# Seven packed blocks and a ring that grows, for six blocks and a fixed ring

## The chip, the core and the metric

The kernel runs on one core of a Trainium2 chip. A core has a matrix engine (PE, TensorE), a vector engine (DVE, VectorE), a scalar engine (ACT, ScalarE), GpSimd (POOL) and a sync engine (SP), and 16 DMA engines that move data between HBM and the on-chip memory SBUF. All DMAs of this kernel are issued from the queues of SP (loads) and of ACT (stores). The metric is the device time of one execution in microseconds (us).

## The reference

The input x has 384 x 384 positions of 384 channels in bf16, 113.25 MB. The kernel needs the mean and the maximum of every channel over all positions, passes both through a small two-layer network, and multiplies x by the sigmoid of the result:

```python
xf = x.reshape(B, H * W, C)
gap = jnp.mean(xf, 1)
gmp = jnp.amax(xf, 1)
h_a = gap @ w1;  h_a = h_a * (h_a > 0)
h_m = gmp @ w1;  h_m = h_m * (h_m > 0)
scale = sigmoid(h_a @ w2 + h_m @ w2)
return x * scale[:, None, None, :]
```

The scale is known only when all of x has been read, and x does not fit in SBUF. So x is read once for mean and maximum (pass one), and what could not be kept is read again, multiplied and stored (pass two).

## The kernel before

The 147,456 positions are spread over the 128 partitions, 1152 on each. "A row" is one of those 1152: 384 channels, 768 B on each partition, 98,304 B over all. Blocks are stretches of consecutive rows, and a partition's part of a block is contiguous in HBM.

**Pass one.** `steps` lists loads and work in order, and one loop issues them in that order on every engine; nothing reorders them (`manual_schedule`). For each load, PE adds the rows up by matmuls with a column of ones (`sums`, L253), and VectorE takes the running maximum in `acc`, in pieces of 6 and 5 rows (`maximum`, L319). Most loads go to a ring of three slots of 39 rows (`SLOT`, `SLOTS`). A slot is loaded anew when VectorE and PE are both done with its last content, and as SP issues in order, a load that waits for its slot holds back all loads behind it.

**Packed blocks.** Six blocks of 32 rows (`PACKED`, `G = 8`: four parts of 8 rows) are kept in the place of 24 rows. The low bytes of the third and fourth part move to where the high bytes of the first and second were, and the high bytes of all four are squeezed to four bits each: matmuls with scaled identity matrices write them as 16-bit words into PSUM, and ScalarE evicts those words into the third part. For each block, in two halves, the order is: load 24 rows into `homes[i]` and 8 rows into `fourth[i]`, `test` (ScalarE, L280 and L281: do the values fit four bits?), `pack` first half (24 matmuls L301, two ScalarE copies L307, an eviction L308), more `test`, the first fill between the blocks, and then `pack` second half. PE's second pack needs the eviction of the first, because both use the PSUM tile `words`. `BETWEEN` says which fills of the slots come after each block (108 rows, so 140 with the block), `PASSING` which come after all blocks, and `judge` turns the tests into one flag. If a value did not fit, the packed rows are read again at the very end (`tc.If(bad != 0)`); with these inputs that is not taken.

**What stays.** The last loads of pass one remain in place: 120 rows in the slots (`STAYING`), 21 in `held` (`LAST_HELD`), and 18 in PSUM. Together with 192 packed rows, pass two has to read 790 rows again (`AGAIN`), and 8 + 11 rows of `held` and `acc` while the scale is computed.

**Pass two.** The rows that stayed are multiplied and stored in small pieces (`FIRST_STORES`). The 120 rows of the ring become four places of 30 rows (`PLACE`); as a place's rows have been stored, SP reads the next 30 into it. A turn is: multiply one place (L416), store it from ACT's queue (L469), issue the read that follows in the same place (L492), and do one job of `jobs`: unpack half a block (VectorE L447 and L452, then six ScalarE copies L466) or multiply a finished block (`finish`). Block 0 is stored as soon as it is finished and its place is used as scratch; blocks 1 to 5 stay in `room` and are stored in the last three turns and after them.

Two orders matter for what follows. Stores are issued from ACT's queue, so a store stands behind the ScalarE copies of the job before it. And the DMA completions are counted on eight semaphores in rotation: a DMA waits for the one eight before it in the program.

Of the kernel before, what the change touches and what calls it, by code (L numbers as in the profile page):

```python
# [12 lines left out]
BF16 = mybir.dt.bfloat16  # L13
# [14 lines left out]

SLOT = 39
SLOTS = 3
RING = 120
PLACE = 30
G = 8
PACKED = 6
PSUM_ROWS = 8
LATE_ROWS = 8
BANK_ROWS = 2
# [1 line left out]
HELD_ROWS = 21  # L41
# [2 lines left out]

FIRST_LOAD = 4
FOLD_BEFORE = 2
BETWEEN = ((18, 36, 33),) + ((36, 36, 36),) * 4 + ((38, 37, 33),)
PASSING = (31, 29, 26, 23, 16, 22, 16)
SHARED_FILL = 4
STAYING = {0: (11, 17, 11), 1: (14, 13, 12), 2: (11, 9, 6, 5, 6, 5)}  # L50
LAST_HELD = (5, 4, 6, 6)

AGAIN = (30,) * 26 + (10,)
FIRST_STORES = ((1, 2, 3, 4, 4, 6, 6, 6, 7), (12, 13, 14), (20, 22))
HELD_STORES = (6, 7)
ACC_STORES_AT = 3
TEST_SCALE = 0.031187
# [5 lines left out]
def kernel(  # L63
# [7 lines left out]
    nc = tc.nc  # L71
    P = nc.NUM_PARTITIONS
# [4 lines left out]
    TOT = HW // P  # L77
# [19 lines left out]
    def take(n):  # L97
        nonlocal at
        at += n
        return at - n, n  # L100
# [10 lines left out]
    assert at == TOT and sum(AGAIN) == n_pass and sum(LAST_HELD) == HELD_ROWS  # L111
    at = passing_at
    again = [take(n) for n in AGAIN]


    small = consts.tile([P, 16], BF16)
# [22 lines left out]
    ring = xpool.tile([P, RING, C], BF16, name="ring")  # L139
    slots = [ring[:, SLOT * i:SLOT * i + stay[i][1], :] for i in range(NS)]  # L140
    places = [ring[:, PLACE * i:PLACE * (i + 1), :] for i in range(RING // PLACE)]
    spare = ring[:, SLOT * NS, :]
    room = xpool.tile([P, 3 * G * PACKED, C], BF16, name="room")
    homes = [room[:, 3 * G * i:3 * G * (i + 1), :] for i in range(PACKED)]
    fourth = [held[:, G * (i % 2):G * (i % 2 + 1), :] for i in range(PACKED)]
    tested = held[:, 2 * G:2 * G + G // 2, :].rearrange("p n c -> p (n c)").bitcast(U8)
    tests = held[:, 2 * G + G // 2, :].bitcast(F32)
# [283 lines left out]
            nc.scalar.dma_start(out=acc_rows(orr, lo, hi), in_=acc[:, lo:hi, :])  # L431

    turns = len(AGAIN)
    homes_d = [held[:, G:2 * G, :], held[:, 0:G, :], held[:, G:2 * G, :], acc[:, 0:G, :], room[:, 0:G, :], room[:, G:2 * G, :]]
    HG = G // 2
    m = held[:, 2 * G:2 * G + HG, :]
    t = acc[:, G:G + HG // 2, :].rearrange("p n c -> p (n c)").bitcast(U8)
# [1 line left out]
    def unpack(i, h):  # L441

        u16 = lambda rows: rows.rearrange("p n c -> p (n c)").bitcast(U16)
        u32 = lambda rows: rows.rearrange("p n c -> p (n c)").bitcast(U32)

        def scalars(dst, src, s1, op0, s2, op1):
            nc.vector.tensor_scalar(out=u16(dst), in0=u16(src), scalar1=s1, scalar2=s2, op0=op0, op1=op1)  # L447

        def nibbles_to_bytes(v):
            scalars(m, v, 3, ALU.logical_shift_right, 0x0101, ALU.bitwise_and)  # L450
            scalars(m, m, float(0x8F), ALU.mult, 0.0, ALU.add)
            nc.vector.scalar_tensor_tensor(  # L452
                out=u32(v), in0=u32(v), scalar=0x3F3F3F3F, in1=u32(m), op0=ALU.bitwise_xor, op1=ALU.bitwise_xor
            )
# [30 lines left out]
    jobs += [[], [(finish, PACKED - 1)]]  # L485

    order = []

    def read_into(buf):
        if again:  # L490
            b = again.pop(0)
            nc.sync.dma_start(out=buf[:, 0:b[1], :], in_=rows_of(xr, b))  # L492
            order.append((b, buf))

    k = ACC_STORES_AT
    put(stay[0], slots[0], FIRST_STORES[0][:k])
# [5 lines left out]
    read_into(places[0])  # L502
    put(stay[1], slots[1], FIRST_STORES[1])
    read_into(places[1])
    put(stay[2], slots[2], FIRST_STORES[2])
    read_into(places[2])
    read_into(places[3])
    nc.vector.tensor_scalar(out=flag, in0=bad_ps, scalar1=0.5, scalar2=None, op0=ALU.is_gt)
    bad = nc.values_load(flag, engines=(ENG.SP, ENG.Activation, ENG.DVE))
    assert len(jobs) <= turns - 4  # L510
    step = 3 * G * 2
    after = [
        [(room[:, 3 * G:3 * G + step, :], 3 * G)],
        [(room[:, 3 * G + step:3 * G + 2 * step, :], 3 * G + step)],
        [(held[:, 0:2 * G, :], d_at + G), (homes_d[3], d_at + 3 * G), (room[:, 0:2 * G, :], d_at + 4 * G)],
    ]
    last = places[(turns - 1) % len(places)][:, AGAIN[-1]:, :]
    leaving = []
    for turn in range(turns):
        b, buf = order.pop(0)  # L520
        multiply(buf[:, 0:b[1], :], buf[:, 0:b[1], :])
        if turn >= turns - len(after):
            for rows, lo in after[turn - turns + len(after)]:
                store(rows, packed_block, lo)
        store(buf[:, 0:b[1], :], b, 0)
        read_into(buf)
        for job, *which in jobs.pop(0) if jobs else ():
            job(*which)
        if turn == turns - 3:
            j = 0  # L530
            for block, rows in ((held_block, late), (ps_block, kept_ps[:, 0:PSUM_ROWS, :]), (beside, kept_b)):
                n = rows.shape[1]
                to = last[:, j:j + n, :]
# [4 lines left out]
                j += n  # L538
            for to, block, rows in leaving[1:] + leaving[:1]:
                multiply(to, rows)  # L540
    assert not again and not order
    for to, block, rows in leaving:
        store(to, block, 0)
    store(homes[PACKED - 1], packed_block, 3 * G * (PACKED - 1))
# [37 lines left out]
```

## Time and profile before

| what | value |
|---|---|
| times of the runs | 731.14, 729.51, 729.61 us; median 729.61 |
| profiled execution | 730.09 us, its span 728.3 us |
| HBM read, written | 192.92 MB, 113.25 MB |
| busy, us: VectorE, ScalarE, PE | 553.2, 300.1, 174.0 |
| last load of pass one landed | 270.40 us |
| scale ready, first store issued | 277.4, 277.9 us |
| first read of pass two issued | 291.1 us |
| last read landed | 677.6 us |
| VectorE idle before pass-two multiplies | 89.5 us, 86.7 of it for reads to land |

The page gives the busy time of each engine, then the span in 40 slices with a digit of tenths for each, then the DMA queues (q1 carries SP's loads, q10 ACT's stores), the chain of work that ended last, and the costliest groups of instructions. Matmuls overlap, so a busy PE need not be a full one. The row for windows gives, for each engine, busy time and number of instructions, then the granted PE clock as a share, the busy share of the DMA engines and their rate.

### The profile page before, as it was taken

The numbers are of one execution on the slowest core, as the hardware profiler recorded it, in microseconds if no ns is written. First come the engines' busy times: TensorE is split into PE (matmuls) and PEld (weight loads), VectorE is DVE, ScalarE is ACT, GpSimd is POOL, SyncE is SP. The second block draws the span as 40 slices with busy tenths as digits, with TensorE's granted clock in tenths as the row PEclk, the third lists the DMA queues.
The fourth block names the chain that finished last, engine by engine and source line by source line (L and its number), as shares of the span: only waits on it lengthen the run. The fifth ranks groups of instructions, "written<-read, shape, count | busy, mean of one in ns | idle before, by whom it ended". The sixth has DMA issues, their size and how long they took to land.

```text
span 728.3 us, 3675 instructions
## 1 busy us (share of the span) xinstructions
PE 174.0 (24%) x1303; PEld 68.6 (9%) x1303; DVE 553.2 (76%) x406; ACT 300.1 (41%) x218; POOL 0.7 (0%) x6
## 2 busy tenths in 40 slices
PE   5576757567644570000000000000000000001000
PEld 1222313222211140000000000000000000001000
DVE  5799999999999998968966989798885554357100
ACT  6999999999910000044443360615340000000000
POOL 0000000000000000000000000000000000000000
PEclk9988889897875555555555555555555555555555
DMA  9999999999999979999999999999999999999997
GB/s 378 432 432 419 436 434 432 421 430 431 425 430 421 420 302 363 391 429 436 426 431 428 438 430 428 439 429 429 437 428 437 433 426 440 430 426 435 444 417 337
DMA packets 21411, 306.41 MB, mean 421 GB/s; under 512 B 2736, under 2 KB 3344, under 8 KB 8336
## 3 DMA queue, kind: packets, MB, share of 16 engines
q1 hardware_dynamic: 13184, 192.93, 62.4%
q10 hardware_dynamic: 8208, 113.25, 36.4%
q8 instruction: 10, 0.16, 0.1%
q14 instruction: 9, 0.07, 0.0%
HBM read 192.92 MB, written 113.25 MB: 420 GB/s over the span
## 4 chain that ended last, share of the span: by engine, by line
DMA 64%; DVE 26%; issue 2%; ACT 0%; SPq 0%; PE 0%; DVEq 0%; ACTq 0%
DMA ring<-in_x_dram 40%; DMA out_dram<-ring 20%; DVE acc L319 13%; DVE ring L416 9%; DMA out_dram<-room 4%; DVE room L416 1%; DVE held L416 1%; DVE held L447 1%; SPq L350 0%; DVE room L447 0%; DVE room L452 0%; DVE acc L452 0%; ACT held L466 0%; DVE acc L416 0%; ACT room L466 0%
## 5 line engine op out<-in xcount | busy, mean ns | idle before, releaser
L416 DVE TENSOR_TENSOR ring<-ring,scale_bc 128x11520 bf16<-128x11520 bf16 (+12 forms) x41 | 187.5, 4595 | 89.5 <-DMA ring<-in_x_dram 86.7
L319 DVE TENSOR_TENSOR acc<-acc,ring 128x1920 bf16<-128x1920 bf16 (+3 forms) x184 | 202.1, 1171 | 14.6 <-DMA ring<-in_x_dram 14.6
L253 PE MATMUL bank_a<-ring,small 128*1 128x512 bf16 (+2 forms) x741 | 81.4, 484 | 78.5 <-DMA ring<-in_x_dram 78.5
L325 PE MATMUL words_ps<-ident_bf,ring 128*128 128x128 bf16 x24 | 2.7, 313 | 382.9 <-DVE ring L535 382.9
L281 ACT ACTIVATE held<-held 128x3072 uint8<-128x3072 uint8 (+1 forms) x30 | 70.3, 2344 | 1.0
L466 ACT COPY room<-room 128x1536 uint8<-128x1536 uint8 x28 | 40.9, 1474 | 48.0 <-DVE ring L416 42.6
L280 ACT ACTIVATE held<-room,held 128x3072 uint8<-128x3072 int8 (+1 forms) x24 | 53.1, 2211 | 6.5 <-DMA room<-in_x_dram 6.1
L466 ACT COPY held<-room 128x1536 uint8<-128x1536 uint8 x8 | 11.7, 1474 | 89.6 <-DVE ring L416 69.5
L253 PEld LDWEIGHTS <-small 128*1 128x1 bf16 x885 | 31.3, 97 | 160.7 <-issue 146.4
L325 PEld LDWEIGHTS <-ring 128*128 128x128 bf16 x24 | 2.5, 147 | 383.3 <-DVE ring L535 383.3
L416 DVE TENSOR_TENSOR room<-room,scale_bc 128x9216 bf16<-128x9216 bf16 (+1 forms) x8 | 33.0, 4151 | 0.0
L466 ACT COPY acc<-room 128x1536 uint8<-128x1536 uint8 x16 | 23.5, 1469 | 23.0 <-DVE ring L416 20.5
L301 PE MATMUL words_ps<-room,scale_bc 128*128 128x512 fp8e4 (+1 forms) x108 | 30.4, 392 | 7.0 <-ACT room L308 7.0
L319 DVE TENSOR_TENSOR acc<-acc,room 128x2304 bf16<-128x2304 bf16 (+2 forms) x28 | 29.0, 1100 | 0.0
L263 ACT COPY w_sb<-bank_a 65x128 f32<-65x128 f32 x2 | 0.5, 262 | 63.5 <-PE bank_a L253 63.0
L466 ACT COPY room<-acc 128x1536 uint8<-128x1536 uint8 x16 | 23.6, 1473 | 0.4
L301 PE MATMUL words_ps<-room,w_sb 128*128 128x512 fp8e3 x72 | 21.5, 380 | 0.0
L301 PE MATMUL words_ps<-held,ring 128*128 128x512 fp8e4 x72 | 21.4, 379 | 0.0
L452 DVE SCALAR_TENSOR_TENSOR room<-room,held 128x768 uint32<-128x768 uint32 x20 | 19.2, 959 | 0.7
L447 DVE TENSOR_SCALAR room<-room 128x1536 uint16<-128x1536 uint16 x20 | 11.1, 557 | 10.6 <-DMA out_dram<-room 10.2
L307 ACT COPY room<-held 128x1536 uint8<-128x1536 uint8 x12 | 17.6, 1470 | 0.0
L307 ACT COPY room<-room 128x1536 uint8<-128x1536 uint8 x12 | 17.5, 1460 | 0.0
(73 smaller groups left out, 205.0 us busy)
## 6 DMA issues: line engine op xcount, KB each, us to landing
ring<-in_x_dram SPq DMA_DIRECT2D x26, 2880.0 KB, 22.7
out_dram<-ring ACTq DMA_DIRECT2D x26, 2880.0 KB, 25.6
ring<-in_x_dram SPq DMA_DIRECT2D x13, 3456.0 KB, 24.1
room<-in_x_dram SPq DMA_DIRECT2D x5, 2304.0 KB, 29.2
out_dram<-room ACTq DMA_DIRECT2D x2, 4608.0 KB, 37.9
ring<-in_x_dram SPq DMA_DIRECT2D x2, 3168.0 KB, 28.6
held<-in_x_dram SPq DMA_DIRECT2D x7, 768.0 KB, 30.5
out_dram<-room ACTq DMA_DIRECT2D x2, 2304.0 KB, 25.9
```

What stands on the lines that cost most here:

```text
L253: nc.tensor.matmul(sum_ps[q * QP:q * QP + 1, 0:g * P], lhsT=ones_bf[:, 0:1], rhs=rows[:, k:k + g, q * P:(q + 1) * P], start=(done + k == 0 ...
L263: nc.scalar.copy(out=s_sb[r % 2], in_=sum_ps[:, r * P:(r + 1) * P])
L280: nc.scalar.activation(out=out_, in_=rows, func=ACT.Square, bias=test_bias, scale=TEST_SCALE)
L281: nc.scalar.activation(out=out_, in_=out_, func=ACT.Square, bias=minus4, accum_out=tests[:, k:k + 1],)
L301: nc.tensor.matmul(words[:, c:c + BANK], lhsT=weights[2 * r + k], rhs=high(part(i, r), dt)[:, half * n + c:half * n + c + BANK], start=(r ...
L307: nc.scalar.copy(out=high(part(i, r), U8)[:, span], in_=low(part(i, r + 2), U8)[:, span])
L319: nc.vector.tensor_tensor(out=out_, in0=in0, in1=in1, op=ALU.max)
L325: nc.tensor.transpose(out=out_[:, r, q * P:(q + 1) * P], in_=rows[:, r, q * P:(q + 1) * P], identity=ident_bf)
L416: nc.vector.tensor_tensor(out=dst, in0=src, in1=scale_bc.unsqueeze(1).to_broadcast([P, n, C]), op=ALU.mult)
L447: nc.vector.tensor_scalar(out=u16(dst), in0=u16(src), scalar1=s1, scalar2=s2, op0=op0, op1=op1)
L452: nc.vector.scalar_tensor_tensor(out=u32(v), in0=u32(v), scalar=0x3F3F3F3F, in1=u32(m), op0=ALU.bitwise_xor, op1=ALU.bitwise_xor)
L466: nc.scalar.copy(out=dst, in_=src)
```

## The change

- `PACKED` goes from 6 to 7: 224 rows are kept packed instead of 192.
- The slots go from 39 to 31 rows (`RING` 96 for 120). Slots and packed blocks now lie in one tile, `body`: rows 0 to 95 are the ring, and block i has the 24 rows from 96 + 24 i.
- `BETWEEN` is cut to fills of 31 rows, four and three in turn: 156, 125, 156, 125, 156, 125 rows for each block with its fills, and (30, 27) after the seventh. `PASSING`, `STAYING` and `LAST_HELD` are new to match; the last two loads have 4 and 6 rows for 6 and 6.
- Pass two reads 782 rows in 25 turns. Where each read goes is written out in `PLACES` (first row, number of rows): four places of 24 rows at first, then 30, 36 and 48 as packed blocks leave.
- `finish(i)` stores its block at once (`store_block`), except the last one. A read is issued when the turns whose rows it covers have passed, and when the blocks in its place have been finished (`read`); the read itself waits for their stores to land.
- The scratch `f` is always in `acc`, and the fourth part of block i is unpacked into one of two places in `held` in turn (`homes_d`), where that of block i - 2 was.
- At the end come the three stores of `leaving`, block 6, and the last read's rows.

```diff
-SLOT = 39
+SLOT = 31
-RING = 120
-PLACE = 30
+RING = 96
-PACKED = 6
+PACKED = 7
...
-BETWEEN = ((18, 36, 33),) + ((36, 36, 36),) * 4 + ((38, 37, 33),)
-PASSING = (31, 29, 26, 23, 16, 22, 16)
-SHARED_FILL = 4
-STAYING = {0: (11, 17, 11), 1: (14, 13, 12), 2: (11, 9, 6, 5, 6, 5)}
-LAST_HELD = (5, 4, 6, 6)
-
-AGAIN = (30,) * 26 + (10,)
-FIRST_STORES = ((1, 2, 3, 4, 4, 6, 6, 6, 7), (12, 13, 14), (20, 22))
+BETWEEN = (
+    (10, 31, 31, 31), (31, 31, 31), (31, 31, 31, 31), (31, 31, 31), (31, 31, 31, 31), (31, 31, 31), (30, 27),
+)
+PASSING = (25, 22, 21, 10, 17)
+SHARED_FILL = 2
+STAYING = {0: (16, 15), 1: (11, 10, 10), 2: (10, 9, 4, 6, 5)}
+LAST_HELD = (6, 5, 4, 6)
+PLACES = (
+    (0, 24), (24, 24), (48, 24), (72, 24), (0, 24), (24, 24), (48, 24), (72, 24), (96, 24),
+    (0, 30), (30, 30), (60, 30), (90, 30), (120, 24), (0, 36), (36, 36), (72, 36), (108, 36), (144, 48),
+    (0, 48), (48, 48), (96, 48), (144, 36), (192, 30), (0, 20),
+)
+FIRST_STORES = ((1, 2, 3, 4, 4, 5, 6, 6), (9, 10, 12), (16, 18))
...
-    homes_d = [held[:, G:2 * G, :], held[:, 0:G, :], held[:, G:2 * G, :], acc[:, 0:G, :], room[:, 0:G, :], room[:, G:2 * G, :]]
+    homes_d = [held[:, G * ((i + 1) % 2):G * ((i + 1) % 2 + 1), :] for i in range(PACKED)]
...
-        f = room[:, 2 * G:2 * G + HG, :] if i > 1 else acc[:, 0:HG, :]
+        f = acc[:, 0:HG, :]
...
-        if i == 0:
-            store(homes[0], packed_block, 0)
-            store(homes_d[0], packed_block, d_at)
+        if i < PACKED - 1:
+            store_block(i)
...
-    jobs = [[(unpack, 0, 0)], [(unpack, 0, 1), (unpack, 1, 0)], [(finish, 0)], [(unpack, 1, 1)]]
-    for i in range(2, PACKED):
+    jobs = [[(unpack, 0, 0)], [(unpack, 0, 1)]]
+    for i in range(1, PACKED):
         jobs += [[(unpack, i, 0)], [(finish, i - 1)], [(unpack, i, 1)]]
     jobs += [[], [(finish, PACKED - 1)]]
...
+    def read(last_turn, blocks_gone):
+        if not again:
+            return False
+        k = len(PLACES) - len(again)
+        lo, n = PLACES[k]
+        if lo + n > RING + 3 * G * blocks_gone or max(turn_of_row[lo:lo + n]) > last_turn:
+            return False
+        turn_of_row[lo:lo + n] = [k] * n
+        buf, b = body[:, lo:lo + n, :], again.pop(0)
+        nc.sync.dma_start(out=buf, in_=rows_of(xr, b))
+        order.append((b, buf))
+        return True
...
     for turn in range(turns):
         b, buf = order.pop(0)
-        multiply(buf[:, 0:b[1], :], buf[:, 0:b[1], :])
-        if turn >= turns - len(after):
-            for rows, lo in after[turn - turns + len(after)]:
-                store(rows, packed_block, lo)
-        store(buf[:, 0:b[1], :], b, 0)
-        read_into(buf)
+        multiply(buf, buf)
+        if turn == turns - 1:
+            for to, block, rows in leaving:
+                store(to, block, 0)
+            store_block(PACKED - 1)
+        store(buf, b, 0)
+        while read(turn, gone):
+            pass
         for job, *which in jobs.pop(0) if jobs else ():
             job(*which)
+            gone += job is finish
```

More of the change, by code (lines that the diff above doesn't have):

```diff
@@ L46 @@
 FOLD_BEFORE = 2
[L47 to L54 removed]
+BETWEEN = (
[6 more added lines that the diff above has]
+PLACES = (
[3 rows of a table added]
+)
+LEAVING_AT = 222
+FIRST_STORES = ((1, 2, 3, 4, 4, 5, 6, 6), (9, 10, 12), (16, 18))
 HELD_STORES = (6, 7)
@@ L110 @@
     passing = [take(n) for n in PASSING]
-    assert at == TOT and sum(AGAIN) == n_pass and sum(LAST_HELD) == HELD_ROWS
+    assert at == TOT and sum(n for _, n in PLACES) == n_pass and sum(LAST_HELD) == HELD_ROWS
     at = passing_at
-    again = [take(n) for n in AGAIN]
+    again = [take(n) for _, n in PLACES]
     small = consts.tile([P, 16], BF16)
@@ L138 @@
     held = nc.alloc_sbuf_tensor_at("held", [P, HELD_ROWS, C], BF16, offset=RING_BYTES).ap()
[L139 to L144, printed above, removed]
+    body = xpool.tile([P, RING + 3 * G * PACKED, C], BF16, name="body")
+    slots = [body[:, SLOT * i:SLOT * i + stay[i][1], :] for i in range(NS)]
+    spare = body[:, SLOT * NS, :]
+    homes = [body[:, RING + 3 * G * i:RING + 3 * G * (i + 1), :] for i in range(PACKED)]
     fourth = [held[:, G * (i % 2):G * (i % 2 + 1), :] for i in range(PACKED)]
@@ L431, in put_acc @@
             nc.scalar.dma_start(out=acc_rows(orr, lo, hi), in_=acc[:, lo:hi, :])
-    turns = len(AGAIN)
-    homes_d = [held[:, G:2 * G, :], held[:, 0:G, :], held[:, G:2 * G, :], acc[:, 0:G, :], room[:, 0:G, :], room[:, G:2 * G, :]]
+    turns = len(PLACES)
+    homes_d = [held[:, G * ((i + 1) % 2):G * ((i + 1) % 2 + 1), :] for i in range(PACKED)]
     HG = G // 2
@@ L476, in finish, with store_block @@
             multiply(rows, rows)
-        if i == 0:
-            store(homes[0], packed_block, 0)
-            store(homes_d[0], packed_block, d_at)
-    jobs = [[(unpack, 0, 0)], [(unpack, 0, 1), (unpack, 1, 0)], [(finish, 0)], [(unpack, 1, 1)]]
-    for i in range(2, PACKED):
+        if i < PACKED - 1:
+            store_block(i)
+    def store_block(i):
+        store(homes[i], packed_block, 3 * G * i)
+        store(homes_d[i], packed_block, d_at + G * i)
+    jobs = [[(unpack, 0, 0)], [(unpack, 0, 1)]]
+    for i in range(1, PACKED):
         jobs += [[(unpack, i, 0)], [(finish, i - 1)], [(unpack, i, 1)]]
@@ L487 @@
     order = []
[L489 to L493, printed above, removed]
+    turn_of_row = [-1] * (RING + 3 * G * PACKED)
+    def read(last_turn, blocks_gone):
[7 more added lines that the diff above has]
+        buf, b = body[:, lo:lo + n, :], again.pop(0)
+        assert b[1] == n
+        nc.sync.dma_start(out=buf, in_=rows_of(xr, b))
+        order.append((b, buf))
+        return True
     k = ACC_STORES_AT
@@ L501 @@
     put(refill, held[:, 0:LATE_ROWS, :], (LATE_ROWS,))
-    read_into(places[0])
+    read(-1, 0)
     put(stay[1], slots[1], FIRST_STORES[1])
-    read_into(places[1])
+    read(-1, 0)
     put(stay[2], slots[2], FIRST_STORES[2])
-    read_into(places[2])
-    read_into(places[3])
+    read(-1, 0)
+    read(-1, 0)
     nc.vector.tensor_scalar(out=flag, in0=bad_ps, scalar1=0.5, scalar2=None, op0=ALU.is_gt)
     bad = nc.values_load(flag, engines=(ENG.SP, ENG.Activation, ENG.DVE))
[L510 to L517, printed above, removed]
+    assert len(jobs) <= turns - 2
     leaving = []
+    gone = 0
     for turn in range(turns):
         b, buf = order.pop(0)
-        multiply(buf[:, 0:b[1], :], buf[:, 0:b[1], :])
-        if turn >= turns - len(after):
-            for rows, lo in after[turn - turns + len(after)]:
-                store(rows, packed_block, lo)
-        store(buf[:, 0:b[1], :], b, 0)
-        read_into(buf)
+        multiply(buf, buf)
[6 more added lines that the diff above has]
+            pass
         for job, *which in jobs.pop(0) if jobs else ():
             job(*which)
+            gone += job is finish
         if turn == turns - 3:
-            j = 0
+            j = LEAVING_AT
+            assert j >= max(lo + n for lo, n in PLACES) and gone > PACKED - 2
             for block, rows in ((held_block, late), (ps_block, kept_ps[:, 0:PSUM_ROWS, :]), (beside, kept_b)):
                 n = rows.shape[1]
-                to = last[:, j:j + n, :]
+                to = body[:, j:j + n, :]
                 if block == held_block:
@@ L538 @@
                 j += n
+            assert j <= RING + 3 * G * (PACKED - 1)
             for to, block, rows in leaving[1:] + leaving[:1]:
@@ L541 @@
     assert not again and not order
-    for to, block, rows in leaving:
-        store(to, block, 0)
-    store(homes[PACKED - 1], packed_block, 3 * G * (PACKED - 1))
     with tc.If(bad != 0):
```

## The prediction

> **What bounds the kernel now.** I read the page first: the busy shares, then the slices, then the chain that ended last.
>
> ```profile
> span 728.3 us, 3675 instructions
> PE 174.0 (24%) x1303; PEld 68.6 (9%) x1303; DVE 553.2 (76%) x406; ACT 300.1 (41%) x218; POOL 0.7 (0%) x6
> ...
> DMA  9999999999999979999999999999999999999997
> ...
> q1 hardware_dynamic: 13184, 192.93, 62.4%
> q10 hardware_dynamic: 8208, 113.25, 36.4%
> ...
> DMA 64%; DVE 26%; issue 2%; ACT 0%; SPq 0%; PE 0%; DVEq 0%; ACTq 0%
> ```
>
> No compute engine is full, and the DMA row is nine tenths or more in 38 of 40 slices. So bytes set the time, and a microsecond is gained only by moving fewer rows or lost by leaving the DMA engines dry. (A row is one of the 1152 of a partition: 768 B by 128, 98,304 B.) The chain of waits in order of time gives the price of a row in both passes:
>
> ```profile
> 60.75 7.78 DVE acc L319 x7
> ...
> 68.59 24.05 DMA ring<-in_x_dram
> ...
> 601.81 22.72 DMA ring<-in_x_dram
> ...
> 624.56 6.17 DVE ring L416
> ...
> 630.75 25.57 DMA out_dram<-ring
> ...
> 656.37 21.24 DMA ring<-in_x_dram
> ```
>
> Pass one: a slot goes round in 7.78 + 24.05 + 0.2 = 32.0 us while 140 rows are loaded: 0.2285 us a row. Pass two: from 601.81 to 656.37, 54.56 us, four turns of 30 rows read and 30 written: 0.2273 us a row. Neither loop is a latency: in each the DMA part is mostly queueing behind other transfers. The stretches by engine say the same, and where it is not so:
>
> ```profile
> 10.00:203.00 193.00, 129.11 (x921) 49.13 (x916) 179.02 (x167) 190.27 (x128) 0.00 (x0) 0.88 1.01 430
> 203.00:270.00 67.00, 36.07 (x288) 13.00 (x288) 66.32 (x63) 1.28 (x7) 0.00 (x0) 0.56 0.98 407
> 270.00:279.00 9.00, 4.26 (x64) 3.52 (x62) 6.90 (x13) 0.83 (x3) 0.00 (x0) 0.69 0.61 223
> 279.00:291.00 12.00, 0.00 (x0) 0.00 (x0) 12.00 (x11) 0.00 (x0) 0.00 (x0) 0.50 0.97 382
> ```
>
> The columns are PE, PEld, DVE, ACT, POOL, clock, DMA share, GB/s. ScalarE is busy 190 of 193 us while blocks are packed: it needs 32.1 us a block (starts at 74.41, 106.52 and so on), and 140 rows of DMA take 32.0. The two are level, with nothing to spare.
>
> **The change, part by part.** The sum starts from the profiled execution, 730.09 us (span 728.3), 0.5 above the median 729.61.
>
> *Fewer reads.* 32 more rows are kept packed, 24 fewer in the slots; pass two reads 782 rows for 790. 8 x 0.2273 = -1.8 us. All of it lies on the DMA path.
>
> *Last pieces.* The last two loads of pass one have 4 and 6 rows for 6 and 6. Both maxima come after the fold, in the serial stretch before the scale: 1.37 (6 rows) against 0.95 us (4 rows). -0.4.
>
> *A seventh block: engine time.* ScalarE +32.1 us in pass one (idle from 203 to 266), 12 copies of 1.474 us in pass two; VectorE 12 operations of 0.557, 4 of 0.96 and nothing to multiply anew (10.5 us), beside 89.5 us of idle time before its pass-two multiplies; PE 48 matmuls of 0.215 (10.3 us), beside 78.5 us idle before its sums. The VectorE maxima are the same 232 instructions on the same elements in another mix. Nothing, as long as the queues stay fed; without that cover VectorE's 10.5 and ScalarE's 17.7 us would show in pass two. The terms of block 6 and of the ring ask that.
>
> *Pass one at block 6.* Rows loaded per block are now 156, 125, 156, 125, 156, 125, against ScalarE's steady 32.1 us. A block's first rows came at 170.38 for block 5, after 724 rows:
>
> ```profile
> 170.38 2.72 PE L253 MATMUL bank_a<-room,small 128*1 128x512 bf16 x18 [1.51 <-DMA room<-in_x_dram]
> ...
> 180.88 2.22 PE L253 MATMUL bank_a<-ring,small 128*1 128x512 bf16 x30 [1.87 <-DMA ring<-in_x_dram]
> ...
> 183.99 0.81 PE L301 MATMUL words_ps<-room,scale_bc 128*128 128x512 fp8e4 x3 [0.89 <-ACT room L308]
> ...
> 189.32 2.17 PE L253 MATMUL bank_a<-ring,small 128*1 128x512 bf16 x30
> ```
>
> By rows, block 6 lands at 170.4 + 143 x 0.2285 = 203.0. ScalarE starts block 1 when it lands (42.2 now, 16 rows later 45.8) and then works five blocks on end: 45.8 + 5 x 32.1 = 206.5, 3.5 late. PE's second pack waits for ScalarE's eviction of the first, 13.3 us after that start as in block 5 (170.73 to 183.99): 219.8. Behind it in PE's queue stand the sums of the next fill (27 rows, landed 217.9), and that slot is reloaded only after them. Loads after it wait in SP's queue, and now no further block is left to cover: the DMA queue runs dry when the 22-row load lands at 203.0 + 112 x 0.2285 = 228.6. With 2.2 us from issue to first bytes (the 8-row reload of held: 4.02 less 8 x 0.2285) the issue is due at 226.4. PE needs 24 matmuls at 0.215 (5.2 us) and 1.5 us of sums: 226.5 at full clock. But PE has then been idle 5.8 us, and after each idle stretch of 5.4 us or more in this phase the sums run at half pace: 27 in 4.00 us at 164.87, where 30 take 2.22 at 180.88. The granted clock came back 2.9 to 4.2 us after work began in four such places, after 8.5 to 8.9 in two. So 228.3 (3.6 us at 0.43 a matmul, then 15.6 matmuls) or, at worst, 230.8. Lost: 0.1, 1.9 or 4.4 us; bounds 0 (ScalarE less late than I reckon) and 4.4. I take 2.3: the six precedents of that idle length, four to two, give 2.7, and there is some chance of no gap. Blocks 2 and 4 are as late, but 32 rows of the next block in the queue (7.3 us) cover it.
>
> The Trainium skill (TensorE: Matmul & The Clock Gate, Part 1: The HAM clock gate) says that one idle window of about 3.4 us halves the clock and about 3.4 us of sustained work restores it. By that rule the pack takes 3.4 us slow and 16.1 matmuls fast, 6.9 us, and the loss is 1.8 us. The trace agrees in four of six cases; in the other two PE paused again before it was warm.
>
> *More, smaller loads.* 59 loads for 57 in pass one; a 5-row load lands 1.19 to 1.25 us after the one before, 0.05 to 0.1 over its rows. +0.1 to +0.2; I take 0.1.
>
> *Start of pass two.* The first read needs 25 stored rows instead of 32, so it starts some 1.6 us sooner. In 279 to 291 the stores alone reached 382 GB/s. 1.6 x (432 - 382)/432 = -0.2; it reaches to -1.0 if the slack of 291 to 330 (410 GB/s) shrinks too.
>
> *The ring.* Early turns have four places of 24 rows, 96 for 120. Each turn has 48 rows of DMA, 10.9 us; over three turns a block's 32 rows come on top: 40 us for three turns, against VectorE 3 x 4.95 + 2 x 5.3 + 6.7 = 32.1. A new wait: the first copy of `unpack(i,0)` writes where block i-2's fourth part still leaves, so ScalarE stands until that store lands, and behind it in ScalarE's queue stand the turn's store and block i-1's. When it is freed the two stores issued before it (48 rows) and a started read (16) are still to move, 64 rows or 14.6 us, against 8.8 us for six copies: 5.7 us in hand. The same wait of 18.9 us exists once now, at 375 to 394, and the slices there show no dip (424 and 443 GB/s). 0 to +4; I take 0.3.
>
> *The end.* Stores drain a full queue before and after: 0. The last read is landed long before.
>
> Sum: 730.09 - 1.8 - 0.4 + 2.3 + 0.1 - 0.2 + 0.3 = 730.4; less 0.5 for the median, 729.9.
>
> **The rivals.**
>
> A, PE is in time (late ScalarE absorbed or full clock), the reads start as reckoned or better: 729.9 - 2.3 = 727.6, down to 726.8 with all of the start's gain. For it: at full clock the issue is only 0.1 us late. Against it: six of six idle stretches of that length. Only its lower part is faster by more than 0.3% (2.2 us, about what a measurement of this kernel can tell from no change).
>
> B, slower: pass two runs dry in turns 4 to 10. It happens if, when ScalarE is let go, less than 8.8/0.2273 = 39 rows are left in both queues. A ledger by hand may misjudge that by the 25 rows in hand, and the wait now comes five times, not once. Two or three gaps of 1.5 us: +4, 734. For it: VectorE is 94% used in the first turns (10.2 of 10.9 us). Against it: the DMA share in ten-microsecond slices stays at 0.96 or more from 280 to 720, also around the 18.9 us wait.
>
> C, the clock stays low through the pack: +2.0, 732.
>
> That the reads do not shrink is excluded: the row counts are fixed in the program.
>
> **How the numbers follow.** Forecast case 0.50 (727.4 to 731.8; predicted 729.9); A's lower part 0.18; B 0.20 and C 0.12 slower. Range 726.8 (all gains, no stall) to 734 (B), which leaves out the far ends of A and B. Faster 0.18, same 0.50, slower 0.32.
>
> **What would show it.** Bytes read 192.14 MB for 192.92. ScalarE's seventh block starts some 3.5 us after its rows land, near 206.5. Between 219 and 235 the sums behind the pack start late, the load of 21 rows is issued near 228.3, and VectorE waits for it; DMA falls under 400 GB/s there. Pass one's last load lands 1 to 3 us later than 270.4. From 330 on the DMA share stays at 0.96 or more. The forecast is wrong if that dip is missing (A), or if windows between 350 and 470 fall below 415 GB/s (B).

## The result, and the profile after

The changed kernel took 735.08 us (median of 5 runs, 734.42 to 736.17) against 730.30 us for the kernel before on the same chip: a ratio of 1.0067, 95% interval 1.0052 to 1.0082. It is slower by 4.8 us. The forecast was 729.9 with a range of 726.8 to 734.0, and the time lies outside that range. The profiled execution took 735.08 us, span 733.3. (A ratio below is not the quotient of the two medians: single executions of the kernel before at 736 to 739 us enter it, so a median that is 1.1 us longer can stand beside a ratio of 1.0001.)

The page of the changed kernel, the same parts as were shown of before:

```profile
span 733.3 us, 3860 instructions
PE 187.4 (26%) x1357; PEld 74.5 (10%) x1357; DVE 563.3 (77%) x421; ACT 348.7 (48%) x251; POOL 0.7 (0%) x6
...
DMA  9999999999998988999999999999999999999996
...
q1 hardware_dynamic: 13328, 192.14, 62.0%
q10 hardware_dynamic: 8640, 113.25, 36.3%
...
DMA 54%; DVE 18%; another core or an unknown queue 9%; ACT 7%; PE 5%; issue 2%; SPq 0%; ACTq 0%; DVEq 0%
```

The bytes read are those announced (192.14 MB), and no compute engine came near to full. Two things are new: PE and ACT are in the chain that ended last (5 and 7%; 0 before), and the DMA row has an 8 in slice 13. The stretches by engine (columns PE, PEld, DVE, ACT, POOL, clock, DMA share, GB/s) show where:

```profile
203.00:220.00 17.00, 12.07 (x73) 4.32 (x73) 16.38 (x17) 16.90 (x13) 0.00 (x0) 0.74 1.00 428
220.00:230.00 10.00, 10.00 (x60) 3.79 (x61) 10.00 (x10) 9.87 (x7) 0.00 (x0) 0.76 0.72 307
230.00:240.00 10.00, 4.60 (x54) 1.66 (x48) 7.01 (x7) 9.11 (x9) 0.00 (x0) 0.76 1.00 382
240.00:273.00 33.00, 18.79 (x163) 7.58 (x155) 32.44 (x31) 0.95 (x4) 0.00 (x0) 0.50 0.99 404
```

From 220 to 230 the DMA share is 0.72 and PE is busy for all 10 us: loads wait for PE. That is the stall at block 6, where it was foretold. Its steps in the timeline of PE (start, busy, what, and in brackets the idle time before):

```profile
214.19 1.79 PE L258 MATMUL bank_a<-body,small 128*1 128x512 bf16 x24
219.80 1.44 PE L306 MATMUL words_ps<-body,scale_bc 128*128 128x512 fp8e4 x3 [3.83 <-ACT body L313]
...
227.57 4.16 PE L258 MATMUL bank_a<-body,small 128*1 128x512 bf16 x60
```

The second pack begins at 219.80 (219.8 was reckoned), after an idle stretch and at half pace (three matmuls in 1.44 us), and the sums behind it start at 227.57. The load of 21 rows is issued at 229.07, after the 22-row load has landed (228.78), and lands at 237.09, 3.5 us later than its 21 rows need. Pass one's last load lands at 273.41 instead of 270.40.

Pass two is the surprise. The same windows for both kernels over the 400 us in its middle, before first:

```profile
320.00:720.00 400.00, 2.74 (x24) 2.48 (x24) 259.12 (x134) 101.96 (x71) 0.00 (x0) 0.50 1.00 431
```

```profile
320.00:720.00 400.00, 2.72 (x24) 2.48 (x24) 272.16 (x146) 116.23 (x82) 0.00 (x0) 0.50 1.00 431
```

Both move 431 GB/s at a share of 1.00, so the 16 engines were kept busy on the mean. (SP's own queue of reads was empty more often, counted from issue to landing: for 34 of the 320 us between 320 and 640, against 7 before; stores alone moved meanwhile.) And yet first store to last landing took 450.7 us (281.20 to 731.92) against 448.4 (277.86 to 726.25), with 8 rows less to move. The loss shows at the very end. Two-microsecond windows, the last of before and then those of after:

```profile
722.00:724.00 2.00, 0.00 (x0) 0.00 (x0) 0.00 (x0) 0.00 (x0) 0.00 (x0) 0.50 0.86 369
724.00:726.00 2.00, 0.00 (x0) 0.00 (x0) 0.00 (x0) 0.00 (x0) 0.00 (x0) 0.50 0.30 129
726.00:728.30 2.30, 0.00 (x0) 0.00 (x0) 0.00 (x0) 0.00 (x0) 0.00 (x0) 0.50 0.01 4
```

```profile
722.00:724.00 2.00, 0.00 (x0) 0.00 (x0) 0.00 (x0) 0.00 (x0) 0.00 (x0) 0.50 1.06 452
724.00:726.00 2.00, 0.00 (x0) 0.00 (x0) 0.00 (x0) 0.00 (x0) 0.00 (x0) 0.50 0.79 338
726.00:728.00 2.00, 0.00 (x0) 0.00 (x0) 0.00 (x0) 0.00 (x0) 0.00 (x0) 0.50 0.34 143
728.00:730.00 2.00, 0.00 (x0) 0.00 (x0) 0.00 (x0) 0.00 (x0) 0.00 (x0) 0.50 0.13 54
730.00:733.30 3.30, 0.00 (x0) 0.00 (x0) 0.00 (x0) 0.00 (x0) 0.00 (x0) 0.50 0.03 14
```

A share of 0.13 is two of sixteen DMA engines. In the trace every DMA has 16 completions; they are read here as one for each engine, which the trace does not name, but which fits: two of them come after 728.3, where the share is that of two engines. Those of the last store, in order, us:

```
before 724.0 724.1 724.1 724.1 724.2 724.3 724.3 724.8 725.0 725.2 725.8 725.9 725.9 726.0 726.2 726.3
after  725.7 725.9 725.9 725.9 726.0 726.0 726.1 726.1 726.2 727.6 727.6 728.0 728.3 728.3 731.1 731.9
```

By this reading fourteen engines are through by 728.3, and two work alone until 731.9. From here on "lag" is the last of these sixteen less their mean: 1.24 us before, 4.63 after. The mean engine finished 446.1 us after the first store (447.15 before), so it did gain 1.1 us of the 1.8; the slowest one lost 2.3.

### The profile page after: what moved, and what is told of

It is laid out like the page before. It is cut to its first block, busy times and chain, and to the rows that moved or that the text cites. A ratio compares the mean times of both kernels' runs of the same rounds, so it can differ in the third digit from the quotient of the medians.

```text
span 733.3 us, 3860 instructions
## 1 busy us (share of the span) xinstructions
PE 187.4 (26%) x1357; PEld 74.5 (10%) x1357; DVE 563.3 (77%) x421; ACT 348.7 (48%) x251; POOL 0.7 (0%) x6
## 3 DMA queue, kind: packets, MB, share of 16 engines
q1 hardware_dynamic: 13328, 192.14, 62.0%
HBM read 192.14 MB, written 113.25 MB: 416 GB/s over the span
## 4 chain that ended last, share of the span: by engine, by line
DMA 54%; DVE 18%; another core or an unknown queue 9%; ACT 7%; PE 5%; issue 2%; SPq 0%; ACTq 0%; DVEq 0%
DMA body<-in_x_dram 32%; DMA out_dram<-body 22%; DVE acc L324 8%; DVE body L421 8%; PE words_ps L306 4%; ACT body L312 2%; ACT held L285 2%; ACT held L286 1%; PE bank_a L258 1%; ACT body L313 1%; DVE held L421 0%; ACT body L470 0%; ACT held L470 0%; DVE acc L421 0%
## 5 line engine op out<-in xcount | busy, mean ns | idle before, releaser
L421 DVE TENSOR_TENSOR body<-body,scale_bc 128x9216 bf16<-128x9216 bf16 (+15 forms) x45 | 214.7, 4803 | 106.4 <-DMA body<-in_x_dram 103.6
L324 DVE TENSOR_TENSOR acc<-acc,body 128x2304 bf16<-128x2304 bf16 (+4 forms) x210 | 229.8, 1166 | 17.3 <-DMA body<-in_x_dram 17.3
L470 ACT COPY held<-body 128x1536 uint8<-128x1536 uint8 x14 | 20.6, 1475 | 201.4 <-DMA out_dram<-held 130.6
L258 PE MATMUL bank_a<-body,small 128*1 128x512 bf16 (+2 forms) x849 | 85.6, 453 | 67.4 <-DMA body<-in_x_dram 67.4
L285 ACT ACTIVATE held<-body,held 128x3072 uint8<-128x3072 int8 (+1 forms) x28 | 61.9, 2211 | 10.3 <-DMA body<-in_x_dram 9.8
L306 PE MATMUL words_ps<-body,scale_bc 128*128 128x512 fp8e4 (+1 forms) x126 | 40.4, 436 | 24.4 <-ACT body L313 24.4
L470 ACT COPY body<-acc 128x1536 uint8<-128x1536 uint8 x28 | 41.2, 1472 | 0.4
L306 PE MATMUL words_ps<-body,w_sb 128*128 128x512 fp8e3 x84 | 28.1, 419 | 0.0
L306 PE MATMUL words_ps<-held,body 128*128 128x512 fp8e4 x84 | 27.3, 409 | 0.0
L470 ACT COPY body<-body 128x1536 uint8<-128x1536 uint8 x14 | 20.7, 1475 | 0.4
L312 ACT COPY body<-body 128x1536 uint8<-128x1536 uint8 x14 | 20.4, 1460 | 0.0
```

Source lines behind the costliest of these rows:

```text
L258: nc.tensor.matmul(sum_ps[q * QP:q * QP + 1, 0:g * P], lhsT=ones_bf[:, 0:1], rhs=rows[:, k:k + g, q * P:(q + 1) * P], start=(done + k == 0 ...
L285: nc.scalar.activation(out=out_, in_=rows, func=ACT.Square, bias=test_bias, scale=TEST_SCALE)
L306: nc.tensor.matmul(words[:, c:c + BANK], lhsT=weights[2 * r + k], rhs=high(part(i, r), dt)[:, half * n + c:half * n + c + BANK], start=(r ...
L312: nc.scalar.copy(out=high(part(i, r), U8)[:, span], in_=low(part(i, r + 2), U8)[:, span])
L324: nc.vector.tensor_tensor(out=out_, in0=in0, in1=in1, op=ALU.max)
L421: nc.vector.tensor_tensor(out=dst, in0=src, in1=scale_bc.unsqueeze(1).to_broadcast([P, n, C]), op=ALU.mult)
```

## The experiments

Two questions: is the stall at block 6 what the prediction says it is, and what makes the last DMA engines lag? Every lag below is that of one profiled execution. "Time" is the median, with the difference to the kernel before on the same chip.

**The groups of fills swapped** (pass one alone; run twice):

```diff
-    (10, 31, 31, 31), (31, 31, 31), (31, 31, 31, 31), (31, 31, 31), (31, 31, 31, 31), (31, 31, 31), (30, 27),
+    (10, 31, 31), (31, 31, 31, 31), (31, 31, 31), (31, 31, 31, 31), (31, 31, 31), (31, 31, 31, 31), (30, 27),
```

> Pass one alone is edited: the groups of fills after the blocks alternate 125, 156, 125, ... rows instead of 156, 125, 156, ..., and block 6 lands after the same 843 rows. Theory 1 (block 6 is packed late because block 1 came 16 rows late and ScalarE then worked without a pause): ScalarE starts block 6 as it lands, near 203 us, the load of 21 rows is issued before the 22-row load lands, the windows between 220 and 240 are back above 400 GB/s, and the last load lands near 270.4 instead of 273.4; time 735.1 - 3 = 732. Rival (the last block stalls wherever it stands, because its second pack has no load of a further block as cover): last load again near 273.4, time 735.1. Pass two is untouched, so if the spread of the 16 DMA engines at its end belongs to the schedule of pass two, the DMA share again tapers over some 6 us at the end; if it was a chance of one execution, it is back at 2 us and the time is near 728.5.

> The kernel with the swapped groups once more, for a second profile of it: if the last block's stall is really gone, pass one's last load lands near 270.5 again; and if the spread of the DMA engines belongs to the growing ring, the DMA share again tapers over some 5 us at the end.

Times 732.31 (+2.0, ratio 1.0036, 1.0019 to 1.0054) and 732.02 (+1.7, 1.0022, 1.0000 to 1.0043). The last load landed at 270.53 and 270.59, ScalarE started block 6 at 204.33 instead of 206.54, the load of 21 rows was issued at 224.71, and the dip is gone:

```profile
220.00:230.00 10.00, 6.02 (x56) 2.41 (x55) 10.00 (x10) 9.84 (x8) 0.00 (x0) 1.00 0.99 417
230.00:240.00 10.00, 6.49 (x52) 2.15 (x52) 10.00 (x11) 6.95 (x8) 0.00 (x0) 0.53 1.03 426
```

So some 3 of the 4.8 us are the stall, and it comes from the order of the groups, not from the seventh block as such. The lag stayed: 3.69 and 4.95 us. It isn't a chance of one execution.

**Four places of 24 rows for the growing ring, and a growing ring of 24-row places** (pass two alone; the second edit writes 33 reads, all of 24 rows but the last of 14, into places up to row 216):

```diff
-PLACES = ( ... (0, 36), (36, 36), (72, 36), (108, 36), (144, 48), (0, 48), (48, 48), ... )
+PLACES = tuple((24 * (k % 4), 24) for k in range(32)) + ((0, 14),)
```

> Pass two alone is edited: every read takes 24 rows and the ring stays at four places (33 turns); blocks still leave as they are finished, ScalarE still waits for the store of block i-2's fourth part and issues stores in bursts. If growth is what costs (more rows outstanding, or reads of 30 to 48 rows, let the 16 DMA engines drift apart): the DMA share falls within some 2 to 3 us at the end instead of 6, time 735.1 - 3.4 = 731.7. If the bursts of stores behind ScalarE's new wait cost it: the taper stays near 6 us, time 735. If four places of 24 are too few for the second half: windows between 500 and 700 under 415 GB/s, time 736 or more.

> Pass two alone is edited: the ring grows as before, to nine places, but every read takes 24 rows (33 turns). If the size of the reads and stores (30 to 48 rows) makes the DMA engines drift apart: taper of 2 to 3 us, time near 731.7, as with the fixed ring. If it is the number of rows outstanding: taper of some 6 us, time near 735, unlike the fixed ring. If it is the bursts of stores: 735 in both.

Fixed ring: 732.17 (+1.9), lag 1.87. Growing with 24 rows: 734.38 (+4.1), lag 3.84. In this pair it is growth, not the size of the DMAs, that goes with the lag; the times say less, as most of their difference arose in pass one (last loads at 270.80 and 273.18). For the fixed ring's profile holds a second lesson: its pass one is that of the changed kernel, and still its last load landed at 270.80. The timeline of its PE:

```profile
219.85 0.81 PE L302 MATMUL words_ps<-body,scale_bc 128*128 128x512 fp8e4 x3 [3.96 <-ACT body L309]
...
225.12 2.98 PE L254 MATMUL bank_a<-body,small 128*1 128x512 bf16 x42
```

The idle time before the pack is the same (3.96 us; 3.83 in the changed kernel), but here the clock stayed up (1.00 from 220 to 230, against 0.76): three matmuls in 0.81 us, the sums at 225.12, the load of 21 rows issued at 226.62 and landed at 234.38 (237.09 in the changed kernel). So the same pass one loses 3.5 us or 0.7 at this load, as the clock happens to stand, and the fixed ring's time mixes two effects and doesn't tell the ring's share.

**Swapped groups, and four places of 30 rows once block 0 has left; the same with three of ScalarE's waits removed:**

```diff
+    + tuple((30 * (k % 4), 30) for k in range(18)) + ((60, 26),)
```

```diff
+    homes_d[4:] = [body[:, RING + 3 * G + G * k:RING + 3 * G + G * (k + 1), :] for k in range(PACKED - 4)]
```

> Pass one as with the swapped groups; in pass two the ring takes block 0's place and then stays at four places of 30 rows (28 turns), as in the kernel before; blocks still leave as they are finished. Theory (loss in pass two = more time per row with 24-row DMAs, plus a spread of the 16 DMA engines that grows with the rows outstanding): after the first third the rate is that of before, the taper at the end is some 2 us, first store to last landing 448.4 - 1.8 + 0.5 = 447 us, time 278.5 + 447 + 3.5 = 729. Rival (bursts of stores behind ScalarE's new wait set the spread): taper stays at 5 to 6 us, time near 732 as with the swapped groups alone.

> The same kernel as the swapped groups with four places of 30, and the fourth parts of blocks 4 to 6 are unpacked into the room that block 1 and 2 left, so that ScalarE no longer waits there for the store of block i-2's fourth part (three waits of the five go). If ScalarE's wait costs nothing, as the prediction's term for the ring said: time within 0.5 us of the kernel that keeps the waits. If it costs through bursts of stores: 1 to 3 us faster, and a shorter taper.

730.46 (+0.2, ratio 1.0003, 0.9994 to 1.0012), lag 2.68; and 730.35 (+0.1, 0.9995, 0.9978 to 1.0012), lag 1.97. Ending the growth at 120 rows is worth about 1.6 us over the swapped groups (732.1 over their 17 runs; 732.02 against 730.46 on the same chip). With the stall this takes back all of the 4.8 us but 0.2. The waits for fourth parts, 117.8 us of ScalarE's time in the first and 36.0 in the second, made no difference. But both stand level with the kernel before, not 1.8 us under it. Where is the gain of the reads?

**The kernel before with one thing changed each time.** Eight rows fewer to read (what lay in their place is multiplied and stored, so those rows of the output are not the product); places of 24 rows, five of them, and four of them:

```diff
+            n = b[1] - (8 if len(again) == 14 else 0)
+            nc.sync.dma_start(out=buf[:, 0:n, :], in_=rows_of(xr, b)[:, 0:n, :])
```

```diff
-PLACE = 30
+PLACE = 24
-AGAIN = (30,) * 26 + (10,)
+AGAIN = (24,) * 32 + (16, 6)
```

> The kernel before with 8 rows fewer to read and nothing else: the thirteenth read of pass two takes 22 of its 30 rows; the other 8 rows of that place are multiplied and stored with what lay there, so those 8 rows of the output are not the product. If a row not read is worth 0.2273 us, as the prediction's first term has it: 730.3 - 1.8 = 728.5. If the end is set by one slow DMA engine and its writes rather than by the rows moved: 730.3.

> The kernel before with one size changed: its ring of 120 rows becomes five places of 24 rows for four of 30 (34 turns, the last of 16 and 6 rows). If smaller DMAs cost time per row by themselves: the fixed-ring and growing-24 kernels were some 10 rows behind after 440 us, so 2 to 2.5 us slower than before, about 732.5. If the rows lag there had to do with the blocks that leave or with ScalarE's waits: no change, 730.3.

> The kernel before with its pass two on 96 rows alone: four places of 24 rows for four of 30 (34 turns), 24 of the 120 rows of the ring unused. If 96 rows keep the DMA engines fed, as the prediction's term for the ring had it (0.3 us): 730.4. If the smaller ring is what eats the gain of the reads: 732.

Eight rows fewer: 728.46, or 1.85 us less than before (ratio 0.9975, 0.9947 to 1.0004); the profiled execution's first store to last landing is 446.1 for 448.4. The interval just reaches 1, but ten of the twelve executions are shorter than the shortest of the 23 of before (729.61). So the price of a row, 0.2273 us, fits. Places of 24: 730.46 (+0.2) with five, 730.25 (-0.1) with four. Neither smaller DMAs nor 96 rows in the ring show a cost.

**Early leaving and ScalarE's waits in the kernel before.** Blocks 0 to 4 are stored as soon as finished; then also the fourth parts of all six blocks in two places in turn:

```diff
-        if i == 0:
-            store(homes[0], packed_block, 0)
-            store(homes_d[0], packed_block, d_at)
+        if i < PACKED - 1:
+            store(homes[i], packed_block, 3 * G * i)
+            store(homes_d[i], packed_block, d_at + G * i)
```

> The kernel before with one part of the change alone: each of blocks 0 to 4 is stored as soon as it is finished, instead of in the last three turns and after them; ring, reads and pass one are those of before. If early leaving by itself costs (lag and rows per us): 731.5 to 732, with a taper of 3 us or more. If it costs nothing: 730.3.

> The reverse: the kernel before with blocks 0 to 4 stored as soon as finished, and with the fourth parts of all six blocks in two places of held in turn, so that ScalarE waits for a store at four blocks instead of one. If the waits start the lag: lag 2.5 us or more and 731.5 to 732. If not: 730.3 to 730.9 as with early leaving alone, lag 1.2 to 1.7 us.

730.85 (+0.35, 1.0014, 0.9994 to 1.0034), lag 1.68; and 731.10 (+1.1, 1.0018, 1.0004 to 1.0033), lag 2.11. Early leaving alone can't be told from nothing. With four waits (97.3 us of ScalarE's time) it costs by 0.04% to 0.33%. Time and lag lie between the two cases of the expectation, so this run does not decide whether waits start the lag.

**Seven blocks the other way round.** With the swapped groups and places of 30, blocks 1 to 5 are kept to the last three turns. (In this kernel the rows of `leaving` overwrite part of block 5, which is then stored as it is; the work is the same.)

> The kernel with the swapped groups and four places of 30, with one part undone: only block 0 leaves as soon as it is finished; of blocks 1 to 5 only the fourth parts leave at once, their 24 rows in the last three turns, as in the kernel before. If stores of blocks in the middle of pass two make the slowest DMA engine lag (2 to 2.7 us behind the mean at the end, 1.2 to 1.6 in kernels that keep the blocks): the lag falls to some 1.5 us and the time to 729.3, so that some of the 1.8 us of fewer reads shows. If the blocks' early leaving costs nothing: 730.4 again.

730.74 (+0.2, 1.0004): no gain. Its profile is of its slowest run (732.68), with a lag of 4.42. Then the growing ring with a small end:

> The kernel with the swapped groups and the growing ring, with its last reads alone edited: instead of 48, 36, 30 and 20 rows in places up to row 222, the last five reads take 30, 30, 30, 30 and 14 rows of the first 120. If the lag of the slowest DMA engine comes from the rows outstanding and is only kept alive by them, the smaller ring brings the engines together again before the end: taper some 3 us, time 730.5 as with four places of 30 from the start. If the lag, once there, stays: taper 5 us, time 732.

```diff
-    (0, 48), (48, 48), (96, 48), (144, 36), (192, 30), (0, 20),
+    (0, 48), (48, 48), (0, 30), (30, 30), (60, 30), (90, 30), (0, 14),
```

732.93 (+2.4), not faster, although the lag fell to 0.79 us. A read of 30 rows that lies across two places of 48 waits for both of their stores, no read landed between 622.7 and 664.0, and the mean share of the engines fell to 0.86 and 0.71:

```profile
650.00:660.00 10.00, 0.00 (x0) 0.00 (x0) 0.00 (x0) 0.00 (x0) 0.00 (x0) 0.50 0.86 367
660.00:670.00 10.00, 0.00 (x0) 0.00 (x0) 5.91 (x1) 0.00 (x0) 0.00 (x0) 0.50 0.71 281
```

The engines were level at the end of this run, but after a stretch with part of them idle: a small lag is no aim by itself. The run doesn't say what a small ring alone would have done, as it held reads back too.

**Seven blocks with the pass two of the kernel before** (swapped groups, four places of 24, block 0's place for fourth parts, blocks stored at the end); the same with early leaving; the first once more, with no wait at all:

```diff
+    homes_d[2:] = [homes[0][:, G * k:G * (k + 1), :] for k in range(3)] + homes_d[:2]
...
+        jobs += [[(unpack, i, 0)], [(finish, i - 1)], [(unpack, i, 1)]] + [[]] * (2 if i == 1 else 0)
```

(the diff of the third; in the first two, blocks 4 to 6 alone use block 0's place)

> Seven blocks with the pass two of the kernel before: swapped groups in pass one; four places of 24 rows throughout (34 turns); block 0's place takes the fourth parts of blocks 4 to 6, so two of ScalarE's waits for a fourth part are left; blocks 1 to 6 are stored in the last four turns. If the seventh block's gain is lost through the early leaving and the waits (read queue empty for 50 us and more in 320 to 640, lag 2 to 5 us): read queue empty some 20 us, lag under 2 us, first store to last landing 448.4 - 1.8 = 446.6, time 278.2 + 446.6 + 3.8 = 728.6. If the seventh block itself eats it (more work between the turns, later start): 730.3.

> The same kernel, but blocks 0 to 5 are stored as soon as each is finished. Early leaving alone separates it from the one before. If early leaving costs as much with seven blocks as the gain of the reads: 730.3, read queue empty for 50 us, lag above 2 us. If not: 728.6.

> Seven blocks stored late on four places of 24, as in the run with the pass two of the kernel before, with the two waits left taken away: the fourth parts of blocks 2 to 4 go to block 0's place, those of 5 and 6 to the places of 0 and 1, and unpacking pauses for two turns after block 0 has left. ScalarE then waits for no store. If these waits upset the order of reads and stores and so start the slow engine's lag: lag under 1.7 us at the end, as in the kernels with six blocks, first store to last landing 446.6, time 728.6, which would beat both kernels. If the lag comes from elsewhere: 730 to 731, lag 2 to 3 us.

731.27 (+1.1, ratio 1.0001, 0.9976 to 1.0027), 730.07 (-0.1, 0.9988, 0.9964 to 1.0011) and 730.28 (+0.3, 0.9994, 0.9982 to 1.0005). None is shown to beat the kernel before, and the three can't be told apart (the interval of the second still reaches the full gain, 0.9975). With every wait for a store gone the lag is still 2.16 us. The emptier queue of reads is not what eats the gain either: in the first and third of these it was empty for 8 and 7 us between 320 and 640, as in the kernel before. In the second the queues ran dry near the end (share 0.91 from 710 to 720, and a lag of 0.59 for that reason), because block 6 was stored in the last turn. So its last stores were moved, and then the waits taken away as well:

```diff
-        if turn == turns - 1:
+        if turn == turns - 4:
+            store_block(PACKED - 1)
+        if turn == turns - 2:
             for to, block, rows in leaving:
                 store(to, block, 0)
-            store_block(PACKED - 1)
```

> The kernel with seven blocks that leave early (swapped groups, four places of 24, block 0's place for fourth parts) with its last stores moved: block 6 is stored four turns before the end instead of in the last turn, and the stores of the rows from PSUM one turn sooner. In the profile before this edit the DMA share was 0.98, 0.91 and 0.88 to 0.95 between 700 and 724, so about 1.5 us were lost there. If that is a loss of every execution and nothing else eats the gain of the reads: 730.1 - 1.5 = 728.6, faster than both kernels. If the end is set by the slowest DMA engine anyway: lag 2 to 3 us and 730.1.

> The same kernel with ScalarE's last waits for fourth parts taken away too (fourth parts of blocks 2 to 4 in block 0's place, two turns of pause). If waits add to the lag: faster than the one before by some 0.5 us, 728.1 to 728.6. If not: the same time.

730.64 (+0.1, ratio 0.9999, 0.9981 to 1.0017), lag 3.01; and 731.09 (+0.6, 1.0003, 0.9985 to 1.0020), lag 2.56. The dry stretch is filled in the first of the two (the windows of its end), and nothing is won:

```profile
710.00:720.00 10.00, 0.00 (x0) 0.00 (x0) 1.34 (x2) 0.00 (x0) 0.00 (x0) 0.53 1.00 424
720.00:722.00 2.00, 0.00 (x0) 0.00 (x0) 0.00 (x0) 0.00 (x0) 0.00 (x0) 0.50 1.01 412
722.00:724.00 2.00, 0.00 (x0) 0.00 (x0) 0.00 (x0) 0.00 (x0) 0.00 (x0) 0.50 1.01 420
724.00:726.00 2.00, 0.00 (x0) 0.00 (x0) 0.00 (x0) 0.00 (x0) 0.00 (x0) 0.50 0.30 123
726.00:728.00 2.00, 0.00 (x0) 0.00 (x0) 0.00 (x0) 0.00 (x0) 0.00 (x0) 0.50 0.05 22
```

That is the second expectation of that run: the last engines set the end here, with the queue full. So none of these accounts for the 1.8 us alone: ring size and DMA size cost nothing in the kernel before, and early leaving, waits and the last stores were taken out of kernels with seven blocks without the gain coming back. (Early leaving and waits together did cost the kernel before 1.1 us by the median.) No version that beats both kernels was found.

Profiled executions side by side, us (the mean engine and its lag are taken at the last store):

| kernel | last load | + to first store | + to mean engine | + lag | time of this execution |
|---|---|---|---|---|---|
| before | 270.40 | 7.46 | 447.15 | 1.24 | 730.09 |
| before, 4 places of 24 | 270.26 | 7.50 | 447.23 | 1.32 | 729.98 |
| before, blocks early | 270.27 | 7.40 | 447.43 | 1.68 | 730.31 |
| before, 8 rows fewer | 270.25 | 7.53 | 445.11 | 1.01 | 727.74 |
| seven, no waits | 270.48 | 7.79 | 446.19 | 2.16 | 730.28 |
| seven, as before | 270.36 | 7.69 | 446.52 | 2.95 | 731.24 |
| seven, early, block 6 sooner | 270.86 | 7.81 | 446.46 | 3.01 | 731.77 |
| seven, places of 30 | 270.65 | 7.80 | 446.29 | 2.68 | 730.72 |
| seven, places of 30, blocks late | 270.42 | 7.69 | 446.85 | 4.42 | 732.68 |
| growing ring, swapped | 270.53 | 7.99 | 445.52 | 3.69 | 730.93 |
| growing ring, swapped, again | 270.59 | 7.80 | 446.62 | 4.95 | 733.13 |
| growing ring of 24-row places | 273.18 | 7.67 | 446.93 | 3.84 | 734.79 |
| after | 273.41 | 7.79 | 446.08 | 4.63 | 735.08 |

All profiles with six blocks have a lag of 1.0 to 2.1. With seven blocks it is 1.9 to 5.0 (3.7 to 5.0 with a growing ring), but for the two whose queues ran dry, and there the mean engine was late instead (449.4 and 452.8). Growth is not the only thing that goes with a long lag: the kernel with the blocks late has 4.42 on a ring of 120 rows. In most of them the mean engine gains only part of the 1.8. The times scatter more as well: 728.9 to 732.6 for places of 30, where the kernel before with five places of 24 lies within 730.1 to 731.3, and the kernel before itself, in the same rounds, within 729.3 to 731.4 in 33 of its 35 executions. So the best run comes near the full gain, and the median does not.

## Why the prediction was wrong, point by point

Against the profiled execution of before, the forecast was +0.3 and the result +5.0.

- *Pass one at block 6* was right in mechanism and place (pack at 219.80 as reckoned, issue at 229.07 for 228.3) and mis-sized: +2.3 was taken, between 0 and 4.4, and the last load came 3.0 later; taking the stall away gave 2.8 to 3.1. Its sum has a slip (45.8 + 5 x 32.1 is 206.3, not 206.5; ScalarE did start at 206.54), which changes little. The pack ran at half and then at full pace, as in the middle case, but the issue came at 229.07 for 228.3, and the load landed 3.2 us over the time of its rows (8.02 less 21 x 0.2285) where 2.2 had been allowed. Two details of the clock were off. PE was idle 3.83 us before the pack, not 5.8, because the sums of an earlier fill ended only at 215.98, so the precedents of 5.4 us or more did not quite apply. And the clock came back 5.1 us after the pack began, between the 2.9 to 4.2 and the 8.5 to 8.9 of the text. The Trainium skill (TensorE: Matmul & The Clock Gate, Part 1: The HAM clock gate) says that the idle window of about 3.4 us is free-running, so that where in it the work falls decides. The traces agree: the same pack began at half pace after 3.83 and after 5.82 us of idle time (changed kernel, growing ring of 24-row places), even after 2.79 (swapped groups with places of 30), and at full pace after 3.96 (fixed ring). So the stall came out at 3.5, 3.1 or 0.7 us at that load (changed kernel, growing ring of 24-row places, fixed ring), and one number was forecast.
- *Fewer reads*, -1.8: the price fits (1.85 for 8 rows in the kernel before), and the bytes are as announced. What failed is the sentence that all of it lies on the path. In kernels with seven blocks it never reached the median.
- *Last pieces*, -0.4: the two maxima did take 2.41 us for 2.81, but last load to first store took 7.79 us, 0.3 more than before. VectorE was not waiting: in the changed kernel its fold ended 0.6 us after the last load had landed, where before both were level. What a shorter last piece saves is lost if the engine comes late to it.
- *Start of pass two*: the first read was issued 11.7 us after the first store for 13.2, or 1.5 sooner where 1.6 was reckoned. Its -0.2 is too small to be seen.
- *The ring*, +0.3 (0 to +4): ScalarE waited 130.6 us in five pieces, as foretold, and the engines did not run dry. Rival B is false by its own sign: no stretch of ten microseconds between 350 and 470 fell below 415 GB/s. That its 734 lies near the 735.08 is chance. But growth cost about 1.6 us at a DMA share of 1.00 (732.1 to 730.46 when the ring stops at 120 rows), which no part of the text had.
- *The end*, "Stores drain a full queue before and after: 0". This is the step that failed. A queue that is full on the mean of 16 engines is not full on each. The lag went from 1.24 to 4.63, +3.4 us, the largest miss of the sum. It was not made in the last microseconds: the nine stores that landed from 701 us on all had a lag of 4.6 to 4.7, where those of before had 1.2 from 681 on.

By the profiled executions: 0.6 more in pass one, 0.7 in the last pieces, 4.0 in pass two (3.4 of lag, 0.6 of the mean engine), less 0.7 by which the stretch after the last landing was shorter: 4.7 us, which is what the sum missed.

So the stall and the growth of the ring make up the slowdown: with the groups swapped and the growth ended all of it but 0.2 us was gone. What the reads should have gained is still missing then. By the table it goes, with seven blocks and no growth, to a first store that is 0.2 to 0.4 us later, a lag that is 0.9 to 3.2 longer, and a mean engine that gains only part. Open stays why the last engines lag more with seven blocks at all. Two things that all these kernels share were not tried alone: the other positions of the blocks in HBM (224 packed rows ahead of the rest for 192), and the seventh block's work between the turns.

## What to carry to other kernels

In a kernel bound by DMA, price the end by the last DMA engine and not by the mean share: look at the last ten microseconds in windows of two, and count how many sixteenths are still at work. More rows in flight did not help here, where the engines were already fed, and went with a longer lag; how they cause it is not shown. A ring that grows has to be paid for by a queue that ran dry before. And where work of a slow engine alternates between light and heavy groups, put the groups so that the last block, the one without a successor to cover it, follows a heavy one and is met on time.

## What the runs showed of the hardware that was not expected

A DMA's 16 completions come apart at the end, by a few late ones, and not always by two. In the changed kernel fourteen of the last store came by 728.3 us and two at 731.1 and 731.9; in the second profile of the swapped groups fourteen by 725.4, two at 729.4 and 730.0. But where block 6 was stored sooner fifteen came by 726.2 and one at 728.1, and in the growing ring of 24-row places thirteen by 728.4 and three at 730.5 to 731.6. The Trainium skill (DMA: Bandwidth & Descriptors, section Latency and other measured facts) says that DMA engines 7 and 15 are usually slower than the others in traces. The first two traces agree in number, two of sixteen, the others do not; no trace here says which engines these are.

The lag also does not grow steadily; it changes in steps and then stands. In the changed kernel it was 4.7 to 4.9 us for all seven stores that landed from 322 to 386 us, 1.6 to 1.9 for the four from 459 to 484, and 4.6 to 4.7 from 701 on. Before, it was 3.1 to 3.3 for the five from 335 to 388, 1.7 to 1.9 from 411 to 656, and 1.2 from 681 on. What makes a step was not tried.
